# A table of 670 urgencies in place of lines of urgency, with an early table load and later small loads

## The chip, the cores and the metric

The kernel runs on one core of a Trainium2 chip. The metric is device time in microseconds from launch to end. Before the change the median of three timed runs is 1019.95 us (1019.66 to 1020.05).

## What is computed

Attention with a threshold, then two MLPs, all in float32 at the interface. Batch 4, 8 heads, 576 positions, head width 64; so 2304 tokens of width 512, and a hidden width of 2048.

```python
scores = scale * np.matmul(q, k.transpose(0, 1, 3, 2))
thresh = np.max(scores, axis=-1, keepdims=True) - tau
scores = np.where(scores >= thresh, scores, -1000000000.0)
attn = np.exp(scores - np.max(scores, axis=-1, keepdims=True))
attn = attn / (np.sum(attn, axis=-1, keepdims=True) + 1e-09)
x = np.matmul(attn, v)                    # to (B * S, H * D)
g = s * np.maximum(x @ moe_w_in, 0.0) ** 2 + b
x = g @ moe_w_out
h = x @ moe2_w_in
out = (h * (1.0 / (1.0 + np.exp(-1.702 * h)))) @ moe2_w_out
```

## The kernel before

**Work.** Attention goes by batch, half of the query rows (256, the last half with the 64 left over) and pair of heads. A tile is 128 queries of one head. For it TensorE forms the scores with k negated and scaled (`scores`, L491), VectorE takes the least of a row (`nm`, L515), ScalarE the exponential (L537), and VectorE masks and sums (L541). In the first two halves ("f32") the result is transposed on TensorE (L552) and evicted by ScalarE; in the other six it is split in two f16 parts by ScalarE and GpSimd (L565, L566) and transposed by a DMA (L568). Then comes the product with v (L636).

Weights arrive as f32 and are brought to the form in which f16 products are exact enough: a cast (`convert`, L774, by ScalarE or VectorE through `copy`, L335 and L339), a shift (L778), a norm of the weights (L812 to L822, on TensorE and VectorE), and a split in two f16 halves with a common scale (`split_w`, L341 and L863). The first 256 rows go through the first MLP in f32 (`pair32` L1004, `bank32` L1036), the other units of 256 rows as three f16 products (`pair` L977, `bank` L1065). The second MLP works on blocks of 512 rows with seven products in place of eight for the first matrix (`hidden7`, L1277; `hidden2`, L1333, for the last block) and plain ones for the second (`rows2`, L1364).

**Order.** The program is straight-line code. The class `Plan` collects steps, each with its engines, its costs in ns, what it reads and writes, and an urgency `prio`. `Plan.run` (L125) goes through time by these costs: whenever an engine is free it takes the ready step of lowest `prio`, and steps that may run on two engines go to the one that would end them first. `emit` then writes the instructions in that order. So every engine works off a fixed order, and an instruction whose input is late holds what stands behind it. SyncE, which issues all DMAs, is one of these queues.

The urgency of a step comes from the table `KN`: for attention from a start and a pace for each half batch (`a0`, `p0`, ...; `attention`, L693), for the MLPs from a start and a pace for each stage (`mlp`, L1382). The steps that a single call of `do`, or a single job of `mlp`, adds have one such value; here they are called a group.

**Parts near the change.** `consts` (L299) loads tau, s and b, one number each for all 128 partitions, ahead of everything. k's scale is made from tau; s and b are used by the first MLP only. `bank_of` (L827) hands out PSUM banks for the MLPs: one, `y`, until the time `wide`, then three in turn. `scale_out` (L921) finds the common scale of an output matrix and splits its 16 slices.

Of the kernel before, what the change touches and what calls it, by code (L numbers as in the profile page):

```python
# [9 lines left out]
F32 = mybir.dt.float32  # L10
# [39 lines left out]
}  # L50

# [22 lines left out]
class Plan:  # L74
# [6 lines left out]
    def __init__(self):  # L81
        self.steps, self.free, self.turns, self.segment = [], {}, {}, 0
        self.prio, self.first, self.bufs = 0.0, 0.0, []

    def add(self, engines, fn, reads=(), writes=(), allocs=None, prio=None, turns=False):
# [6 lines left out]
        op["prio"] = (self.prio if prio is None else prio) - self.first * ("PE" in engines)  # L92
        op["segment"] = self.segment
# [181 lines left out]
def act(cols, psum=False):  # L275
    return cols * 0.834 + (53.0 if psum else 93.0)
# [12 lines left out]
class Kernel:  # L289
# [9 lines left out]
    def consts(self, pool):  # L299
# [28 lines left out]
    def copy(self, dst, src, reads, writes, cols, scale=None, psum=False, also=0, **kw):  # L328

        nc = self.nc  # L330

        def fn(e):
            if e == "DVE":
                if scale is None:
                    nc.vector.tensor_copy(dst(), src())  # L335
                else:
                    nc.vector.tensor_scalar(dst(), src(), scale(), None, ALU.mult)
            elif scale is None:
# [3 lines left out]
        self.plan.add(self.some({"ACT": act(cols, psum) + (93 if callable(scale) else 0), "DVE": dve(cols, True, psum)}, also), fn, reads, writes, **kw)  # L342
# [29 lines left out]
    def prep_qk(self, p):  # L372
# [15 lines left out]
        add({"ACT": act(S) + 93.0}, lambda _: nc.scalar.activation(k.ap, k.ap, AF.Copy, scale=self.qs), [k], [k])  # L388

    def most(self, b, hp, rv):  # L390

        if hp == 0:
            self.mx[b] = self.at("mx", [P, H], F32, 2)
        mx = self.mx[b]
        self.plan.add(
            {"DVE": float(dve(640))},
            lambda _: self.nc.vector.tensor_reduce(
                mx[:, 2 * hp : 2 * hp + 2], rv.ap, AX.X, ALU.max, apply_absolute_value=True
            ),
            [rv], [(mx, hp)],  # L400
        )
# [42 lines left out]
    def prep_v(self, p):  # L444
# [17 lines left out]
        for h in range(2):  # L462
# [3 lines left out]
                {"DVE": dve(376)},  # L466
# [30 lines left out]
    def tile_step(self, p, i):  # L497
# [22 lines left out]
        if plain:  # L520
            add(
                {"POOL": 300.0},
# [3 lines left out]
        else:  # L526
            add(
                {"DVE": 130.0},
# [7 lines left out]
            {"ACT": 624.0},  # L536
# [25 lines left out]
        self.copy(lambda: p16[:, :S], lambda: e.ap, [e], [(p16, 0)], S)  # L562
# [4 lines left out]
        add({"POOL": Shared(pool(MAIN) + pool(H2))}, low, [e, (p16, 0)], [(p16, 1)])  # L567
        add({"SP": (1360.0, 1800.0, 1280.0)}, lambda _: nc.sync.dma_start_transpose(pt(), p16.ap), [p16], [(PT, part)], turns=True)  # L568

    def finish_sums(self, p):  # L570
# [28 lines left out]
        for h in range(2):  # L599
# [7 lines left out]
            self.copy(lambda h=h: rs[h * H2 : (h + 1) * H2], lambda rT=rT: rT.ap, [rT], [(rs, h)], n, psum=True)  # L607
# [85 lines left out]
    def attention(self, pairs):  # L693
# [3 lines left out]
        for n, p in enumerate(pairs):  # L697
# [4 lines left out]
            def do(step, p, i):  # L702
# [3 lines left out]
                plan.prio = at  # L706
                self.lending = p["b"] * NP + p["hp"] < KN["lend"]
# [57 lines left out]
    def convert(self, m, f, which, stage):  # L765
# [8 lines left out]
        self.copy(lambda: tw[:, :, 1], lambda: st[:, 4:2052:4].bitcast(BF16), [st], [tw], 512, also=KN["cast"])  # L774
# [163 lines left out]
    def bias(self):  # L938
# [11 lines left out]
        for i0 in range(KD):  # L950
# [7 lines left out]
            [C, sv["U"]], [sv["b"]],  # L958
# [33 lines left out]
    def pair32(self, u, jp):  # L992
# [22 lines left out]
        if jp % 2 == 0:  # L1015
# [7 lines left out]
            [gt], [(g, k)],  # L1023
# [27 lines left out]
    def bank(self, u, ib):  # L1051
# [6 lines left out]
        for h in range(2):  # L1058
# [16 lines left out]
            if (ib, h) == (0, 0):  # L1075
# [8 lines left out]
                if u["at"] == 0 or u["n"] == KN["fu"]:  # L1084
                    add(self.tiny(2), scale, [sv["U"], (self.ub, b)], [(sv["y"], b)])
# [296 lines left out]
    def mlp(self):  # L1382
# [189 lines left out]
```

## Time and profile before

| | |
|---|---|
| median of the timed runs | 1019.95 us |
| the profiled execution, its own time | 1023.23 us |
| its span, first to last instruction | 1021.5 us |
| TensorE busy | 979.0 us, 96% |
| VectorE, ScalarE, GpSimd busy | 694.9, 622.8, 207.3 us |
| mean granted clock of TensorE | 0.992 |

In the profile PE is TensorE, PEld its weight loads, DVE VectorE, ACT ScalarE, POOL GpSimd, SPq the queue of SyncE. Names are out<-in, L is a line of the kernel, and what stands in brackets is the idle time of that engine just before and what ended it. The clock is the share of full speed that was granted: 1.00 is 2.4 GHz, and a mean below it says that part of the stretch ran at 1.2 GHz. The trace shows each f32 product as two matmuls where the program has one, and a score tile as four.

### The profile page before, as it was taken

To read this page: it belongs to the slowest core of one execution; us is meant where nothing else is said; L and a number is where in the kernel's file an instruction comes from. 1 tells how busy PE (TensorE), PEld (TensorE's weight loads), DVE (VectorE), ACT (ScalarE), POOL (GpSimd) and SP (SyncE) were. 2 spreads that over 40 slices of the span, in tenths; PEclk is the share of its full clock that TensorE was granted. 3 is DMA by queue.
4 is the path that set the end of the run, shared out by engine and by line. 5 is a ranking of instruction groups with operands and counts; after the bars stand their busy time and mean duration, and the time that the engine had idled before them with its cause. 6 is when DMAs were issued, how large, how long until landed. Compare 5 with 4: busy or idle time off the path is not lost.

```text
span 1021.5 us, 21133 instructions
## 1 busy us (share of the span) xinstructions
PE 979.0 (96%) x8181; PEld 723.0 (71%) x8181; DVE 694.9 (68%) x1538; ACT 622.8 (61%) x1194; POOL 207.3 (20%) x319
## 2 busy tenths in 40 slices
PE   5888999979999999999999999999999999999998
PEld 3556667757877777777778888886486486486483
DVE  5888688796778777886675888796366356356240
ACT  5777776587677666676555888694364355354250
POOL 2110034433443454444442000000001001000000
PEclk9999999999999999999999999999999999999999
DMA  7786267736668786776764257310010010000000
GB/s 258 260 287 220 68 167 176 172 66 160 123 136 210 157 165 126 151 169 144 148 105 83 93 175 237 131 49 1 32 53 1 31 53 1 31 32 1 31 12 21
DMA packets 173060, 115.84 MB, mean 113 GB/s; under 512 B 136536, under 2 KB 149920, under 8 KB 172960
## 3 DMA queue, kind: packets, MB, share of 16 engines
q1 hardware_dynamic: 172960, 114.50, 43.8%
q8 instruction: 64, 1.05, 0.4%
q14 instruction: 36, 0.29, 0.1%
HBM read 72.62 MB, written 10.00 MB: 81 GB/s over the span
## 4 chain that ended last, share of the span: by engine, by line
PE 74%; DVE 10%; ACT 7%; DMA 5%; issue 2%; POOL 0%; SPq 0%; ACTq 0%; DVEq 0%; POOLq 0%
PE a L1364 18%; PE yy L1065 11%; PE a L1277 8%; PE yy L977 7%; PE S L491 6%; PE y L977 4%; PE T L636 3%; PE y L1036 3%; PE yy L1277 3%; PE d L1277 2%; DVE e L541 2%; DMA wst<-in_moe_w_out 2%; DMA PT<-p 2%; DVE nm L515 2%; PE y L1277 2%
## 5 line engine op out<-in xcount | busy, mean ns | idle before, releaser
L977 PEld LDWEIGHTS <-wb 128*128 128x128 f16 x1536 | 147.8, 98 | 32.8 <-issue 15.9
L565 POOL TENSOR_TENSOR p<-e,p 128x512 f16<-128x512 f32 x108 | 128.5, 1190 | 204.3 <-ACT p L339 176.6
L1065 PEld LDWEIGHTS <-wb 128*128 128x128 f16 x1536 | 148.5, 98 | 26.7 <-issue 9.3
L1065 PE MATMUL yy<-g,wb 128*128 128x256 f16 x1248 | 146.3, 274 | 2.1 <-DVE g L354 1.7
L541 DVE SCALAR_TENSOR_TENSOR e<-S,tb,e 128x576 f32<-128x576 f32 x144 | 115.0, 814 | 47.4 <-ACT e L537 44.0
L1364 PE MATMUL a<-wb,g 128*128 128x512 f16 x648 | 145.2, 379 | 0.0
L1277 PEld LDWEIGHTS <-l 128*128 128x128 f16 x1344 | 131.5, 98 | 19.2
L515 DVE TENSOR_REDUCE nm<-S 128x1 f32<-128x576 f32 x144 | 104.5, 749 | 29.9 <-PE S L491 29.7
L1364 PEld LDWEIGHTS <-g 128*128 128x128 f16 x648 | 63.4, 98 | 72.1
L537 ACT ACTIVATE e<-S,tb 128x576 f32<-128x576 f32 x108 | 76.4, 735 | 56.7 <-DVE tb L529 47.1
L977 PE MATMUL yy<-xs,wb 128*128 128x256 f16 x888 | 104.2, 273 | 0.0
L1277 PE MATMUL a<-xs,l 128*128 128x256 f16 x768 | 96.4, 273 | 0.0
L339 ACT ACTIVATE p<-e 128x576 f16<-128x576 f32 x108 | 73.0, 677 | 32.9 <-DMA PT<-p 22.8
L977 PE MATMUL y<-xs,wb 128*128 128x256 f16 x648 | 78.6, 273 | 7.3 <-ACT gt L984 7.3
L341 ACT ACTIVATE gt<-a,x2y 128x512 f32<-128x512 f32 x18 | 12.4, 688 | 88.0 <-PE a L1364 64.8
L354 POOL TENSOR_TENSOR st<-wb 128x512 f32<-128x512 f32 x5 | 7.1, 1418 | 276.3 <-DVE gt L1234 123.0
L491 PE MATMUL S<-kk,qa 64*128 64x288 f32 (+1 forms) x320 | 54.6, 445 | 8.2 <-ACT kk L388 8.2
L1229 ACT ACTIVATE gt<-wb,x2h 128x256 f32<-128x256 f32 x64 | 36.4, 609 | 40.4 <-DVE wb L1296 37.8
L491 PE MATMUL S<-kk,qb 64*128 64x288 f32 (+1 forms) x320 | 57.6, 453 | 1.5 <-DVE e L541 1.4
L1289 ACT ACTIVATE wb<-a 128x256 f32<-128x256 f32 x96 | 36.3, 379 | 30.2 <-PE a L1277 29.7
L778 DVE SCALAR_TENSOR_TENSOR wb<-wst,tw 128x512 int32<-128x512 int32 x64 | 45.5, 713 | 6.6 <-ACT tw L339 6.0
L1364 PE MATMUL a<-wb 128*128 128x512 f16 x216 | 49.4, 379 | 0.0
(184 smaller groups left out, 1589.2 us busy)
## 6 DMA issues: line engine op xcount, KB each, us to landing
wst<-in_moe_w_in SPq DMA_DIRECT2D x32, 512.0 KB
wst<-in_moe_w_out SPq DMA_DIRECT2D x32, 512.0 KB
rv<-in_v SPq DMA_DIRECT2D x32, 320.0 KB
kk<-in_k SPq DMA_DIRECT2D x32, 288.0 KB
qb<-in_q SPq DMA_DIRECT2D x16, 288.0 KB
yd<-gt SPq DMA_DIRECT2D x18, 256.0 KB
wb<-yd SPq DMA_DIRECT2D x16, 256.0 KB
out<-gt SPq DMA_DIRECT2D x16, 256.0 KB
```

The costliest lines, as they stand in the source:

```text
L339: nc.scalar.activation(dst(), src(), AF.Copy)
L491: nc.tensor.matmul(Sp[to, half, :HALF], q[h][r, qcols], k[r, h * HALF : (h + 1) * HALF])
L515: {"DVE": 668.0}, lambda _: nc.vector.tensor_reduce(nm.ap, Sv(), AX.XY, ALU.min), [Sp], [nm],
L537: lambda _: nc.scalar.activation(ev(), Sv(), AF.Exp, bias=nm.ap if plain else nb(), scale=-1.0), [Sp, biased], [e],
L541: lambda _: nc.vector.scalar_tensor_tensor(ev(), Sv(), tb(), ev(), ALU.is_le, ALU.mult, accum_out=p["acc"][:, i, 0:1]),
L565: nc.gpsimd.tensor_tensor(p16[:, S + H2 :], e[:, :MAIN], p16[:, :MAIN], ALU.subtract)
L778: lambda _: nc.vector.scalar_tensor_tensor(stage[:, j, :].bitcast(I32), st.ap.bitcast(I32)[:, 1:1025:2], 13, flat(), ALU.logical_shift_rig ...
L977: nc.tensor.matmul(hps[:, h, :], W[:, i, j, kk * P : (kk + 1) * P], x[:, k, kk, :], start=t == 0, stop=t == len(terms) - 1,)
L1065: nc.tensor.matmul(yp[:, h, :], self.W[0, 1, c][:, i, j, i0 * P : (i0 + 1) * P], u["g"][c][:, k, j, :], start=t == 0, stop=t == len(terms) ...
L1229: lambda _, cols=cols, h=h: nc.scalar.activation(gt[:, cols], h(), AF.Tanh, scale=th[:, c : c + 1]),
L1277: nc.tensor.matmul(to(bank), W[:, u, m, j, kk * P : (kk + 1) * P], y[:, v, z, kk, :], start=n == 0 and not more, stop=n == 5, skip_group_c ...
L1364: nc.tensor.matmul(yp(), part(f, k), self.W[1, 1, f // CH][:, w, f % CH, :], start=n == 0, stop=n == 47,)
```

## The change

1. Each group of steps gets an urgency of its own: a table `MOVES` of 670 numbers, in units of 100 ns, one for each group in the order in which the program forms them (the first ones attention's, the later ones those of the MLPs), is added to the value that the line gives. `KN` keeps its lines.
2. Costs of some steps in the plan are changed: the cast of weights and some copies on ScalarE by 50 to 180 ns, the scale of k by 67, the exponential from 624 to 650, `tb` from 130 to 200 on VectorE with a port shared with GpSimd, and others alike. They change the order only.
3. `consts` loads tau only, and calls an exponential on a column of ones, so that ScalarE's table load stands first on it. s and b are loaded by steps of the first `prep_qk`, behind the first k and q; what uses them now waits for a buffer `scal`.
4. Some steps may go to GpSimd (`tp`, `kp`, `mp`); all three switches are 0.

```diff
+MOVES = [
+    -17, -87, -158, 439, -1, -284, -28, 285, -1, 61, -158, -163, -103, -293, -250, -322, -101, 289, 151, 1356, -464,
...
+]
...
+        op["prio"] += 100.0 * MOVES[self.group] if self.group < len(MOVES) else 0.0
+        op["group"] = self.group
...
-        for i, src in enumerate((self.tau, self.s, self.b)):
-            nc.sync.dma_start(sc[:, i : i + 1], src.partition_broadcast(P))
-        self.s_ap, self.b_ap = sc[:, 1:2], sc[:, 2:3]
+        self.scal = Buf(None, "scal", None, None)
+        nc.sync.dma_start(sc[:, 0:1], self.tau.partition_broadcast(P))
+        warm = pool.tile([P, 1], F32, name="warm")
+        nc.scalar.activation(warm, self.ones[:, 0:1], AF.Exp)
+        self.scal_t, self.s_ap, self.b_ap = sc, sc[:, 1:2], sc[:, 2:3]
...
-        add({"ACT": act(S) + 93.0}, lambda _: nc.scalar.activation(k.ap, k.ap, AF.Copy, scale=self.qs), [k], [k])
...
+        engines = {"ACT": act(S) + 160.0}
...
+        add(engines, scale, [k], [k])
+        if p["unit"] == p["hp"] == 0:
+            for i, src in ((1, self.s), (2, self.b)):
+                self.load(lambda i=i: self.scal_t[:, i : i + 1], lambda src=src: src.partition_broadcast(P), [self.scal], P * 4)
...
-                {"DVE": dve(376)},
+                {"DVE": dve(490)},
...
-                {"DVE": 130.0},
+                {"DVE": Shared(200.0)},
...
-            {"ACT": 624.0},
+            {"ACT": 650.0},
...
                 plan.prio = at
+                plan.group += 1
...
             self.plan.prio = t
+            self.plan.group += 1
```

The queue of SyncE at the start of the program, before the change (`kk`, `qa` and `qb` are k and q, `wst` a slice of weights):

```order
L311 DMA scal<-in_tau 128x1
L311 DMA scal<-in_moe_s 128x1
L311 DMA scal<-in_moe_b 128x1
L358 DMA kk<-in_k 128x576
L358 DMA qa<-in_q 128x256
L358 DMA qb<-in_q 128x256
L358 DMA wst<-in_moe_w_in 128x2048
L358 DMA kk<-in_k 128x576
L358 DMA qa<-in_q 128x256
L358 DMA qb<-in_q 128x256
```

and with it:

```order
L350 DMA scal<-in_tau 128x1
L404 DMA kk<-in_k 128x576
L404 DMA qa<-in_q 128x256
L404 DMA qb<-in_q 128x256
L404 DMA scal<-in_moe_s 128x1
L404 DMA kk<-in_k 128x576
L404 DMA qa<-in_q 128x256
L404 DMA qb<-in_q 128x256
L404 DMA wst<-in_moe_w_in 128x2048
L404 DMA scal<-in_moe_b 128x1
```

The first k and q moved up by two places, s behind them, b behind the first weights; the second k and q moved ahead of the first weights.

ScalarE at the same place, before (`tw` is a cast of weights, `e` the exponential, `PT` an eviction of transposed tiles):

```order
L388 ACT_TABLE_LOAD
L388 ACTIVATE kk<-kk,qs 128x576
L339 ACTIVATE tw_78<-wst 128x512
L537 ACTIVATE e<-S,nm 128x576
L388 ACTIVATE kk<-kk,qs 128x576
L537 ACTIVATE e<-S,nm 128x576
L339 ACTIVATE PT_177<-TP 128x4x128
L339 ACTIVATE PT_177<-TP 64x128
```

and with the change:

```order
L352 ACT_TABLE_LOAD
L352 ACTIVATE warm<-ones 128x1
L437 ACTIVATE kk<-kk,qs 128x576 x2
L598 ACTIVATE e<-S,nm 128x576
L382 ACTIVATE tw_78<-wst 128x512
L598 ACTIVATE e<-S,nm 128x576
L382 ACTIVATE PT_178<-TP 128x4x128
L382 ACTIVATE PT_178<-TP 64x128
```

The table load stands alone with its call, and both first copies of k ahead of the first exponential.

TensorE at the norm of the first group of weights, which ends near 84 us, before (`TP` are transpositions, `T` small ones of the sums, L820 the norm's small product, L1004 the f32 matmuls of the first MLP, on the same bank `y`):

```order
L552 MATMUL TP<-ident,e 128x128 x4
L552 MATMUL TP<-ident,e 64x128
L820 MATMUL y<-ident,n_935 128x128
L1004 MATMUL y<-xs,wb 128x256 x4
L552 MATMUL TP<-ident,e 128x128 x4
L552 MATMUL TP<-ident,e 64x128
L605 MATMUL T<-ident,ri 64x128 x2
L491 MATMUL S<-kk,qa 128x288 x2
L491 MATMUL S<-kk,qa 64x288 x2
L491 MATMUL S<-kk,qb 64x288 x2
```

and with the change, where the same lines are L613, L666, L882 and L1066:

```order
L613 MATMUL TP<-ident,e 128x128 x4
L613 MATMUL TP<-ident,e 64x128
L552 MATMUL S<-kk,qa 128x288 x2
L666 MATMUL T<-ident,ri 64x128 x2
L882 MATMUL y<-ident,n_1019 128x128
L613 MATMUL TP<-ident,e 128x128 x4
L613 MATMUL TP<-ident,e 64x128
L666 MATMUL T<-ident,ri 64x128 x2
L1066 MATMUL y<-xs,wb 128x256 x4
L672 MATMUL T<-ident,ri 128x128
L552 MATMUL S<-kk,qa 64x288 x2
```

Transpositions and two small ones now stand between the norm's product and the f32 matmuls.

TensorE at the scale of the last v, near 433 us, before (L416 and L428 turn the maxima of v and spread the scale; rows of weight loads alternate with the matmuls):

```order
L1065 MATMUL yy<-g,wb 128x256
L1065 LDWEIGHTS wb
L1065 MATMUL yy<-g,wb 128x256
L428 MATMUL T<-dg,ones 128x8
L1065 LDWEIGHTS wb
L1065 MATMUL yy<-g,wb 128x256
```

and with the change, the same end of the stretch between them:

```order
L1039 LDWEIGHTS wb
L1039 MATMUL y<-xs,wb 128x256
L1039 LDWEIGHTS wb
L1039 MATMUL y<-xs,wb 128x256
L552 MATMUL S<-kk,qa 128x288 x4
L489 MATMUL T<-dg,ones 128x8
L1039 LDWEIGHTS wb
```

Two score tiles (L552, four matmuls) now stand just ahead of the spread, behind twelve matmuls as before.

## Rows read from the trace of the kernel before

**Rows 1.** Busy time by stretch: us, then each engine's busy time (count), TensorE's clock, DMA.

```profile
0.00:8.17 8.17, 0.00 (x0) 0.00 (x1) 0.62 (x6) 2.06 (x2) 2.71 (x11) 1.00 0.53 165
8.17:100.00 91.83, 78.81 (x495) 50.00 (x497) 78.09 (x174) 70.48 (x141) 11.12 (x35) 0.94 0.78 270
100.00:200.00 100.00, 97.25 (x745) 72.62 (x743) 77.93 (x190) 67.92 (x127) 30.16 (x51) 1.00 0.58 141
200.00:235.00 35.00, 26.17 (x278) 20.24 (x275) 31.37 (x66) 28.16 (x53) 12.59 (x15) 1.00 0.37 73
...
390.00:440.00 50.00, 47.67 (x509) 36.84 (x508) 40.76 (x94) 31.59 (x55) 23.80 (x35) 1.00 0.69 140
...
600.00:650.00 50.00, 47.86 (x438) 42.50 (x437) 40.03 (x73) 40.36 (x83) 1.27 (x1) 1.00 0.58 198
650.00:1000.00 350.00, 350.00 (x2441) 238.70 (x2439) 190.84 (x410) 172.08 (x362) 8.37 (x6) 1.00 0.08 27
1000.00:1021.50 21.50, 16.71 (x78) 7.34 (x76) 0.00 (x0) 1.37 (x2) 0.00 (x0) 0.95 0.11 24
```

**Rows 2.** Whom TensorE waited for, whole span: us in total, times, longest.

```profile
PE y L977 <- ACT gt L984: 7.3, 5, 2.4
...
PE y L1004 <- DVE n L822: 2.7, 2, 2.3
```

**Rows 3.** Timeline of the start: start us, us, engine, line, operation, idle before it.

```profile
1.20 0.42 SPq L311 DMA_DIRECT2D scal<-in_moe_s  x1
...
2.13 0.43 SPq L358 DMA_DIRECT2D kk<-in_k  x1
...
6.05 1.28 ACT L388 ACT_TABLE_LOAD   x1 [6.05 <-DMA kk<-in_k]
...
7.34 0.77 ACT L388 ACTIVATE kk<-kk,qs 128x576 f32<-128x576 f32 x1
...
8.17 2.29 PE L491 MATMUL S<-kk,qa 64*128 64x288 f32 x8 [8.17 <-ACT kk L388]
```

**Rows 4.** Timeline around 84 us, TensorE.

```profile
83.61 0.77 PE L552 MATMUL TP<-ident,e 128*128 128x128 f32 x5
...
84.21 0.27 PE L820 MATMUL y<-ident,n 128*128 128x128 f32 x1
...
86.75 2.89 PE L1004 MATMUL y<-xs,wb 128*128 128x256 f32 x8 [2.27 <-DVE n L822]
```

**Rows 5.** Timeline around 433 us, TensorE.

```profile
431.00 1.47 PE L1065 MATMUL yy<-g,wb 128*128 128x256 f16 x12
...
433.45 0.38 PE L428 MATMUL T<-dg,ones 8*128 8x8 f32 x2 [0.98 <-DVE dg L425]
...
435.95 0.76 PE L491 MATMUL S<-kk,qb 64*128 64x288 f32 x4
```

**Rows 6.** Timeline from 202 to 212 us, all engines.

```profile
202.74 1.16 POOL L565 TENSOR_TENSOR p<-e,p 128x512 f16<-128x512 f32 x1
...
208.44 2.56 ACT L341 ACTIVATE wb<-wb,o 128x512 f16<-128x512 f32 x4 [2.06 <-DVE o L930]
...
210.12 3.63 DVE L863 SCALAR_TENSOR_TENSOR wb<-wb,o 128x512 f16<-128x512 f32 x4
...
211.47 0.57 ACT L984 ACTIVATE gt<-y 128x512 f32<-128x512 f32 x1
...
211.65 1.55 POOL L565 TENSOR_TENSOR p<-e,p 128x512 f16<-128x512 f32 x1 [4.43 <-ACT p L339]
...
212.10 0.82 PE L977 MATMUL y<-xs,wb 128*128 128x256 f16 x6 [2.43 <-ACT gt L984]
```

**Rows 7.** TensorE's groups by line and form: busy us, mean ns, idle before.

```profile
L1004 PE MATMUL y<-xs,wb 128*128 128x256 f32 x128 | 32.0, 396 | 2.7 <-DVE n L822 2.7
...
L812 PE MATMUL y<-wb 128*128 128x128 bf16 x128 | 8.7, 219 | 0.6 <-DVE n L822 0.6
```

**Rows 8.** Busy time by stretch, 75 to 100 us.

```profile
75.00:100.00 25.00, 22.40 (x159) 15.47 (x159) 20.77 (x47) 19.86 (x42) 1.85 (x7) 0.93 0.71 243
```

More of the change, by code (lines that the diff above doesn't have):

```diff
@@ L82, in __init__ @@
         self.steps, self.free, self.turns, self.segment = [], {}, {}, 0
-        self.prio, self.first, self.bufs = 0.0, 0.0, []
+        self.prio, self.first, self.bufs, self.group = 0.0, 0.0, [], -1
     def add(self, engines, fn, reads=(), writes=(), allocs=None, prio=None, turns=False):
@@ L325, in consts, with copy @@
         nc.vector.memset(self.offs[:, 1:2], LOG_SP)
-    def copy(self, dst, src, reads, writes, cols, scale=None, psum=False, also=0, **kw):
+    def copy(self, dst, src, reads, writes, cols, scale=None, psum=False, also=0, wide=False, more=0.0, **kw):
         nc = self.nc
@@ L337, in fn @@
                     nc.vector.tensor_scalar(dst(), src(), scale(), None, ALU.mult)
+            elif e == "POOL":
+                nc.gpsimd.tensor_copy(dst(), src())
             elif scale is None:
@@ L341, in fn @@
                 nc.scalar.activation(dst(), src(), AF.Copy, scale=scale if isinstance(scale, float) else scale())
-        self.plan.add(self.some({"ACT": act(cols, psum) + (93 if callable(scale) else 0), "DVE": dve(cols, True, psum)}, also), fn, reads, writes, **kw)
+        engines = self.some({"ACT": act(cols, psum) + (93 if callable(scale) else 0) + more, "DVE": dve(cols, True, psum)}, also)
+        if wide:
+            engines["POOL"] = pool(cols, True)
+        self.plan.add(engines, fn, reads, writes, **kw)
     def some(self, engines, i):
@@ L387, in prep_qk, with scale @@
             )
-        add({"ACT": act(S) + 93.0}, lambda _: nc.scalar.activation(k.ap, k.ap, AF.Copy, scale=self.qs), [k], [k])
+        def scale(e):
+            if e == "ACT":
+                nc.scalar.activation(k.ap, k.ap, AF.Copy, scale=self.qs)
+            else:
+                nc.gpsimd.tensor_scalar(k.ap, k.ap, self.qs, None, ALU.mult)
+        engines = {"ACT": act(S) + 160.0}
+        if KN["kp"]:
+            engines["POOL"] = pool(S, True)
+        add(engines, scale, [k], [k])
+        if p["unit"] == p["hp"] == 0:
+            for i, src in ((1, self.s), (2, self.b)):
+                self.load(lambda i=i: self.scal_t[:, i : i + 1], lambda src=src: src.partition_broadcast(P), [self.scal], P * 4)
     def most(self, b, hp, rv):
@@ L394, in most @@
         mx = self.mx[b]
+        engines = {"DVE": float(dve(640))}
+        if KN["mp"]:
+            engines["POOL"] = pool(640, True)
         self.plan.add(
-            {"DVE": float(dve(640))},
-            lambda _: self.nc.vector.tensor_reduce(
+            engines,
+            lambda e: self.eng[e].tensor_reduce(
                 mx[:, 2 * hp : 2 * hp + 2], rv.ap, AX.X, ALU.max, apply_absolute_value=True
@@ L561, in tile_step @@
         p16 = self.at("p16", [P, 2 * S], F16, KN["pb"], KN["lp"])
-        self.copy(lambda: p16[:, :S], lambda: e.ap, [e], [(p16, 0)], S)
+        self.copy(lambda: p16[:, :S], lambda: e.ap, [e], [(p16, 0)], S, more=50.0)
         def low(_):
@@ L606, in finish_sums @@
             add({"PE": pe(2 * T, P)}, turn, [ri], [rT])
-            self.copy(lambda h=h: rs[h * H2 : (h + 1) * H2], lambda rT=rT: rT.ap, [rT], [(rs, h)], n, psum=True)
+            self.copy(lambda h=h: rs[h * H2 : (h + 1) * H2], lambda rT=rT: rT.ap, [rT], [(rs, h)], n, psum=True, more=90.0)
         if not p["last"]:
@@ L773, in convert @@
         self.turns += 1
-        self.copy(lambda: tw[:, :, 1], lambda: st[:, 4:2052:4].bitcast(BF16), [st], [tw], 512, also=KN["cast"])
+        self.copy(lambda: tw[:, :, 1], lambda: st[:, 4:2052:4].bitcast(BF16), [st], [tw], 512, also=KN["cast"], wide=KN["tp"], more=180.0)
         flat = lambda: tw.ap.rearrange("p a b -> p (a b)").bitcast(I32)
@@ L1084, in bank @@
                 if u["at"] == 0 or u["n"] == KN["fu"]:
-                    add(self.tiny(2), scale, [sv["U"], (self.ub, b)], [(sv["y"], b)])
+                    add(self.tiny(2), scale, [sv["U"], (self.ub, b), self.scal], [(sv["y"], b)])
         for h in range(2):
```

8 lines of the change are left out of this document (4 added, 4 removed), and 34 rows, old and new, of tables (KN, MOVES).

## The prediction

> **What bounds the kernel now.** I read the table of stretches first [rows 1]. From 650 to 1000 us TensorE is busy 350.00 of 350 us: there the matmuls set the pace, and an order of steps can neither gain nor hide anything. The holes lie ahead of it: 8.17 us before the first matmul, 13.0 us between 8.17 and 100 (91.83 less 78.81), 2.75 between 100 and 200, 8.8 between 200 and 235, 2.3 between 390 and 440, 2.1 between 600 and 650, and 4.8 in the tail, where the last eviction and store follow the last matmul. Together that is 42 of the 42.5 us for which TensorE is idle in the 1021.5 us span. The same table shows the granted clock at 0.94 from 8.17 to 100 us and at 1.00, the level of 2.4 GHz, in the next hundred: 0.06 x 91.83 = 5.5 us of full speed lost to pieces at 1.2 GHz, where TensorE has its holes. From 8.17 to 100 VectorE is busy for 85% of the time (78.09 of 91.83), from 100 to 200 for 78%, and TensorE's idle share falls with it, from 14.2% to 2.75%.
>
> Then the list of who TensorE waited for [rows 2], and the timeline at the places it names. At the start [rows 3] the first k waits in the queue behind three loads of one number each; its landing releases a table load on ScalarE, and only after that is k scaled. At 84 us [rows 4] a small product is put ahead of a group of f32 matmuls that needs the same bank, and TensorE waits 2.27 us for VectorE in between. At 433 us [rows 5] it waits 0.98 us for VectorE's scale of the next v. After 206 us [rows 6] six hidden groups of the first MLP use one bank in turn, and each must be evicted by ScalarE, which has blocks of four weight copies (2.56 us) in its order.
>
> **The change part by part.** The sum is made against the profiled execution (1023.23 us, span 1021.5) and applied to the median of the timed runs, 1019.95; they stand 0.3% apart, which moves a sum of 10 us by 0.03.
>
> *Start: 2.2 us.* The changed order puts k behind tau alone. It takes the slot at 1.20 that the load of s has now, 0.93 us ahead of 2.13 [rows 3]. It landed at 6.05, so 5.12 now. The table load (7.34 less 6.05, 1.28 us) is now released by a constant that GpSimd writes among its first instructions, so nothing stands between the landing and the copy: 5.12 + 0.77 + the 0.06 us hop = 5.95 in place of 8.17. Bounds: 1.28 if the landing does not move, 2.2. The loads of s and b are read by the first MLP alone, much later, and cost a slot of 0.47 us each (half of 0.93) behind the first k and q. The second k's copy now stands before the first exponential on ScalarE; if that k came late the exponential would wait, which is the 0.9 us bound on the other side. By the Trainium skill, "ScalarE: Activation LUTs", What ACT_TABLE_LOAD costs, a table load is followed by a drain and comes to about 2.66 us; the trace shows the copy beginning 7.34 less 6.05 = 1.29 us after the load began, with no drain, so I keep the row. By the page the term would be 1.4 us more and the sum 1009.3.
>
> *The product at 84 us: 0.8 us.* In the new order five transpositions stand between the small product and the f32 group; they take 0.77 us [rows 4] and fill that much of the 2.27 us. Bounds 0 and 2.27.
>
> *The scale of v at 433 us: 1.0 us.* Two score tiles now stand beside the twelve matmuls that fill the wait; one takes 0.76 us [rows 5], so 1.5 us cover the whole 0.98. Bounds 0 and 0.98. The holes of 600 to 650 I leave.
>
> *The f32 attention up to about 140 us: 3.5 us.* Ahead of VectorE's 36th masking product the order now has 171 instructions in place of 187; at 78.09 us for 174 [rows 1] each is 0.45, so 7.2 us of its work goes later. Ahead of TensorE's last f32 transposition stand 16 fewer f32 MLP matmuls and 16 fewer of the weight norm: 16 x 32.0/64, since the trace splits each of the 64 in two, and 16 x 8.7/128 [rows 7], 9.1 us. If VectorE sets the pace, the stretch ends 7.2/0.85 = 8.5 us sooner, and the 9.1 us come back later: +0.6. If the hole follows VectorE's load, as between the two stretches above, 7.2 of some 110 us takes the load from 85 to 79.5% and the idle share from 14.2 to 5.3%, 8.1 us. If the chain of one tile sets the pace, nothing ends sooner and 9.1 us come back. I take the middle of the first two, since the waits are spread over VectorE and ScalarE; bounds -8.1 and +9.1.
>
> *Clock: 1.75 us.* One fall of the clock lies around the 2.27 us hole: 0.93 over 75 to 100 us is 25 x 0.07 = 1.75 [rows 8]. A hole cut to 1.5 us and a stretch with fewer of them should keep this one up. Bounds 0 and the whole 5.5; one fall more would cost 1.75.
>
> *The clump at 206 to 232 us: 0.* Its one bank stays, the four blocks of four copies stay, and on ScalarE the relu of each group still stands behind such a block. Three more score tiles are finished ahead of it, but one more copy of k stands in it. Bounds -7.3 (all waits gone) and +8.4 (below). Two subtractions move from VectorE to GpSimd; beside VectorE's weight subtractions one of GpSimd's takes 1.55 us against 1.16 elsewhere [rows 6], so at most 0.4 us each on an engine nobody waits for, and six casts go from VectorE to ScalarE where both have gaps: nothing. The Trainium skill, "SBUF — State Buffer", Who interferes with whom, has the two engines block each other for whole instructions, which speaks against the move; the trace agrees in direction (1.55 against 1.16). By that rule each of the two could hold VectorE for a whole 1.55 us, 3.1 us in all, and the sum would be 1013.8.
>
> Sum: 2.2 + 0.8 + 1.0 + 3.5 + 1.75 = 9.25 us, so 1019.95 - 9.25 = 1010.7.
>
> **The rivals.** *Only the start is won.* The order shifts holes about: what leaves the f32 stretch comes back later. For it: the moved matmuls are as long (9.1 us) as the time that VectorE saves (8.5). Against it: 100 to 200 us shows that the same mixture runs with 2.75 us of holes. 1019.95 - 2.2 = 1017.7.
>
> *The holes close.* All idle between 8.17 and 200 us goes (15.8), with the clock's 5.5, the start's 2.2 and the 4.4 of 390 to 440 and 600 to 650; the clump stays. 27.9 us, 992. For it: the stretch from 650 to 1000 runs without a hole, with VectorE at 55%. Against it: at 85% VectorE leaves little room, and a tile's chain from score to transposition is as long as before.
>
> *The clump grows: slower.* In it TensorE waited five times for ScalarE, 7.3 us in all [rows 2]. If every group meets a whole block, each wait is 2.56 + 0.57 = 3.13 us [rows 6], 15.7 in all, 8.4 more. With the start's 2.2 and nothing else, 1026. It makes the kernel slower once the five waits pass 9.5 us (1.9 each) if only the start is won, or 16.5 us if everything else comes as summed. For it: relu and block still alternate. Against it: the score tiles finished ahead take work out of this stretch.
>
> **How the numbers follow.** Forecast 47%, its own range 1004 to 1016; only the start 20%; holes close 20%; clump grows 13%. A difference of 0.2% (2.04 us) is about what a measurement of this kernel can tell from none. The start alone is at that edge, so I split it 11 faster and 9 same: faster 0.47 + 0.20 + 0.11 = 0.78, same 0.09, slower 0.13. For the range I leave out half of the closing holes below 995, and most of the growing clump above 1021.
>
> **What would show it.** Right: the first matmul near 5.95 us with the table load at 1 us; a wait under 1.6 us between the norm's small product and the f32 group; TensorE's idle between 8 and 200 us at 9 to 12 us; the clock above 0.95 there; five waits on ScalarE of about 7 us after the weight scale is known; no hole from 650 us on. Wrong: idle of 20 us or more up to 235 us (the order only moved it), waits for relu above 2 us each, or new waits on weight loads. If the last blocks, which now mix hidden groups with output rows, showed holes, the tail would be the step that I did not price.

## The result: slower by 0.6%

The changed kernel takes 1024.37 us (median of five runs, 1022.68 to 1027.16), the kernel before in the same session 1019.66. The ratio is 1.006, 95% interval 1.0041 to 1.0079: 4 to 8 us slower, where 9.25 us less was forecast.

The profile after is of an execution of 1024.37 us. The table of stretches, with the columns and almost the stretches of [rows 1] (core 0: span of the stretch, busy time of PE, PEld, DVE, ACT, POOL, granted clock, DMA share, GB/s):

```profile
0.00:8.17 8.17, 2.29 (x8) 1.19 (x8) 1.38 (x7) 2.84 (x4) 2.89 (x12) 1.00 0.66 186
8.17:100.00 91.83, 78.60 (x524) 47.65 (x524) 80.84 (x180) 73.09 (x146) 14.23 (x37) 0.98 0.77 268
100.00:200.00 100.00, 96.89 (x710) 72.30 (x709) 77.00 (x187) 69.25 (x128) 31.83 (x53) 1.00 0.68 151
200.00:235.00 35.00, 26.90 (x277) 20.65 (x275) 32.56 (x76) 28.25 (x50) 13.58 (x18) 1.00 0.44 93
390.00:440.00 50.00, 50.00 (x517) 39.94 (x516) 35.52 (x94) 33.99 (x60) 23.16 (x32) 1.00 0.72 142
440.00:600.00 160.00, 156.41 (x1546) 128.35 (x1544) 113.52 (x249) 100.44 (x183) 50.26 (x68) 0.99 0.54 122
600.00:650.00 50.00, 48.15 (x436) 42.24 (x434) 42.33 (x78) 37.85 (x78) 5.60 (x4) 1.00 0.55 185
650.00:1000.00 350.00, 350.00 (x2425) 236.66 (x2423) 183.77 (x401) 164.15 (x353) 1.67 (x1) 1.00 0.08 29
```

TensorE's idle time from 8.17 to 200 us is 16.3 us (13.2 and 3.1); it was 15.8. The 2.3 us of 390 to 440 are gone. Between 440 and 600, where it had not stood still at all in the first profile of the kernel before, it now idles 3.6 us; a second profile of the kernel before, shown below, idles 2.3 us there. The list of whom TensorE waited for, to be held against [rows 2] (total us, times, longest):

```profile
PE TP L613 <- ACT PT L382: 6.2, 8, 1.6
PE y L1039 <- ACT gt L1046: 5.8, 5, 2.0
PE yy L863 <- ACT sq L849: 2.0, 1, 2.0
PE y L1211 <- DVE x2t L1208: 1.3, 1, 1.3
```

The wait of 2.27 us at 84 us has left the list, and the five waits on the one bank have shrunk from 7.3 to 5.8. The waits of f32 transpositions for ScalarE's evictions have grown to 6.2 us, from 2.1 and 2.0 in the two profiles of before, and two waits on small products of the second MLP's scales are new (2.0 and 1.3). Around the first of the new ones, TensorE, and below it ScalarE (start us, us, instruction, and in brackets the idle time before it):

```profile
588.65 2.78 PE L1039 MATMUL y<-xs,wb 128*128 128x256 f16 x24
591.27 1.48 PE L1039 MATMUL yy<-xs,wb 128*128 128x256 f16 x12
594.71 0.39 PE L863 MATMUL yy<-fro,ones 128*128 128x4 f32 x2 [1.96 <-ACT sq L849]
594.95 5.76 PE L1127 MATMUL yy<-g,wb 128*128 128x256 f16 x36
```

```profile
591.80 0.79 ACT L382 ACTIVATE tw<-wst 128x512 f16<-128x512 bf16 x1
592.79 0.60 ACT L1046 ACTIVATE gt<-yy 128x512 f32<-128x512 f32 x1 [0.20 <-PE yy L1039]
593.41 0.63 ACT L1047 ACTIVATE gt<-gt 128x512 f32<-128x512 f32 x1
593.95 0.61 ACT L849 ACTIVATE sq<-wb 128x512 bf16<-128x512 f32 x1
```

The small product needs a square of the weights that stands on ScalarE behind a cast and the two steps of an eviction. The 36 matmuls behind the hole take 5.76 us, where at the pace of the 24 in the first line (2.78) they would take 4.2: part of them runs at 1.2 GHz, and the granted clock from 595 to 601 us is 0.72.

### The profile page after: what moved, and what is told of

It is laid out like the page before. It is cut to its first block, busy times and chain, and to the rows that moved or that the text cites. A ratio compares the mean times of both kernels' runs of the same rounds, so it can differ in the third digit from the quotient of the medians.

```text
span 1022.6 us, 21121 instructions
## 1 busy us (share of the span) xinstructions
PE 980.6 (96%) x8181; PEld 721.3 (71%) x8181; DVE 686.5 (67%) x1532; ACT 620.4 (61%) x1199; POOL 211.5 (21%) x321
## 3 DMA queue, kind: packets, MB, share of 16 engines
q8 instruction: 64, 1.05, 0.4%
## 4 chain that ended last, share of the span: by engine, by line
PE 78%; DVE 9%; DMA 5%; ACT 5%; issue 2%; SPq 1%; POOL 0%; DVEq 0%; ACTq 0%; POOLq 0%
PE a L1426 18%; PE yy L1127 10%; PE a L1339 8%; PE S L552 7%; PE yy L1039 7%; PE T L697 5%; PE y L1039 4%; PE y L1127 3%; PE y L1098 3%; PE yy L1339 3%; PE d L1339 2%; PE y L1066 2%; PE y L1339 2%; DVE l L955 2%; PE yy L1395 1%
## 5 line engine op out<-in xcount | busy, mean ns | idle before, releaser
L1039 PEld LDWEIGHTS <-wb 128*128 128x128 f16 x1536 | 148.1, 98 | 33.1 <-issue 15.3
L1039 PE MATMUL yy<-xs,wb 128*128 128x256 f16 x888 | 106.5, 273 | 1.6 <-ACT gt L1046 1.3
L552 PE MATMUL S<-kk,qa 64*128 64x288 f32 (+1 forms) x320 | 55.0, 448 | 6.5 <-ACT kk L437 5.7
L552 PE MATMUL S<-kk,qb 64*128 64x288 f32 (+1 forms) x320 | 57.0, 453 | 3.0 <-DVE e L602 2.9
L1291 ACT ACTIVATE gt<-wb,x2h 128x256 f32<-128x256 f32 x64 | 37.5, 608 | 21.8 <-DVE wb L1358 20.8
L400 DVE TENSOR_TENSOR g<-gt,g 128x512 f16<-128x512 f32 x53 | 43.9, 833 | 8.3 <-ACT g L382 7.8
```

The source lines that it names most:

```text
L552: nc.tensor.matmul(Sp[to, half, :HALF], q[h][r, qcols], k[r, h * HALF : (h + 1) * HALF])
L1039: nc.tensor.matmul(hps[:, h, :], W[:, i, j, kk * P : (kk + 1) * P], x[:, k, kk, :], start=t == 0, stop=t == len(terms) - 1,)
```

## The experiments

Ratios are to the kernel before in the same session (17 to 35 runs of it), with 95% intervals; a ratio that is 0.0001 higher is 0.1 us more. A single execution can lie up to some 8 us from the median of its kernel, the kernel before ranging from 1014.6 to 1029.2 over all sessions.

**A second profile of the kernel before (e0).** No edit.

> The kernel before, unchanged, profiled a second time. Its first profiled execution was 1023.23 us with a span of 1021.5, 3.6 us above the median of the timed runs, so its span beside that of the changed kernel (1022.6) shows a loss of 1.1 us only, where the timed runs show 4 to 5. If the first profiled execution was a long one by chance, this span is about 1017 to 1018 and some hole of the first is smaller. If profiling itself adds 3 us to this kernel, it is 1021 again.

1018.49 us, span 1016.7. So the first profile was a long execution. The second one's stretches from 8.17 to 100 and from 440 to 600 us:

```profile
8.17:100.00 91.83, 81.36 (x522) 50.46 (x523) 79.58 (x178) 73.65 (x146) 12.73 (x36) 0.96 0.79 270
...
440.00:600.00 160.00, 157.74 (x1574) 130.17 (x1572) 115.56 (x255) 105.82 (x191) 47.38 (x68) 1.00 0.58 126
```

In the first it has 10.5 us of idle time in place of 13.0 and a clock of 0.96 in place of 0.94 [rows 1], with the same instructions. In the second it idles 2.3 us, all of them between 580 and 600, where the first profile had none. So that stretch was full in one execution only. The loss of the change is to be read against this one: 5.9 us of span, not 1.1.

**The start alone (e1).** The order of before, the table load early, s and b issued behind the q of the first pair of heads (the code that issues them there is left out):

```diff
-        for i, src in enumerate((self.tau, self.s, self.b)):
-            nc.sync.dma_start(sc[:, i : i + 1], src.partition_broadcast(P))
+        nc.sync.dma_start(sc[:, 0:1], self.tau.partition_broadcast(P))
+        warm = pool.tile([P, 1], F32, name="warm")
+        nc.scalar.activation(warm, self.ones[:, 0:1], AF.Exp)
...
```

> The order of the kernel before, with the early table load and with the two small loads behind the first q. Theory 1 (the start is won and then given back within the first 25 us, because the matmuls run at 1.2 GHz until about 21.7 us in the changed kernel): first S at about 5.8 us, but at 25 us of the span TensorE is only 0.3 to 0.6 us of work ahead, and the time is 0 to 0.6 us under that of before. Rival (the start's 2.4 us stay won wherever the order is the old one): 1017.3 to 1017.7. The other rival (the early start makes the f32 stretch worse): slower by 1 us or more.

The ratio is 1.0001 (0.9986 to 1.0017): nothing is won. The first scores start at 5.75 us, but the first transposition at 13.13, later than the 12.11 of before (second profile). ScalarE's timeline, and then the row of 5 to 7 us, whose last two numbers are the DMA engines' share and GB/s:

```profile
4.93 0.78 ACT L398 ACTIVATE kk<-kk,qs 128x576 f32<-128x576 f32 x1 [2.69 <-DMA kk<-in_k]
10.78 0.77 ACT L341 ACTIVATE tw<-wst 128x512 f16<-128x512 bf16 x1 [5.08 <-DMA wst<-in_moe_w_in]
11.42 0.71 ACT L547 ACTIVATE e<-S,nm 128x576 f32<-128x576 f32 x1
```

```profile
5.00:7.00 2.00, 1.25 (x6) 0.97 (x8) 0.00 (x0) 0.70 (x1) 0.00 (x0) 1.00 0.43 81
```

The cast of the first weight block stands ahead of the first exponential on ScalarE and waits 5.08 us for its load. While the two small loads pass, the queues move 81 GB/s.

**The start with the small loads late (e4).** As e1, against which the diff stands, but s and b are issued behind the second q of the third pair of heads, at 15.3 us:

```diff
-            if h and p["unit"] == p["hp"] == 0:
+            if h and p["unit"] == 0 and p["hp"] == 2:
```

> The start-only kernel again (order of before, early table load), but with the two small loads issued behind the second q of the third pair of heads, some 20 us or more in. Theory 1a (a load of one number to 128 partitions holds up what stands behind it in the queue far longer than the slot of 0.47 us: in the start-only kernel the first weight block landed 2.5 us later than before and held up ScalarE's order): first weight block back at about 8 us or earlier, first transposition at 9.8 to 10.3 us in place of 13.1, time 1016.5 to 1017.5. Rival (the first tiles are bound by matmuls at 1.2 GHz until about 20 us, whatever lands): first transposition earlier, but 1018 to 1019 as the start-only kernel.

The ratio is 0.9966 (0.9945 to 0.9986), faster than both kernels. The same two views:

```profile
4.91 0.78 ACT L398 ACTIVATE kk<-kk,qs 128x576 f32<-128x576 f32 x1 [2.68 <-DMA kk<-in_k]
6.91 0.78 ACT L341 ACTIVATE tw<-wst 128x512 f16<-128x512 bf16 x1 [1.22 <-DMA wst<-in_moe_w_in]
7.91 0.74 ACT L547 ACTIVATE e<-S,nm 128x576 f32<-128x576 f32 x1 [0.22 <-DVE nm L525]
```

```profile
5.00:7.00 2.00, 1.26 (x6) 0.98 (x8) 0.00 (x0) 0.78 (x2) 0.00 (x0) 1.00 1.03 390
```

The block is there 3.9 us earlier, 390 GB/s pass, and the first transposition starts at 9.65. Up to 12 us the queues carry 307 packets under 512 B here and 573 in e1; the two loads of one number to 128 partitions are the only difference between the runs.

**The changed order with either start (e2, e5).** e2 puts the old start under the changed order (the diff of e1 backwards, and the planned loads of s and b issue nothing); e5 is the changed kernel with s and b at e4's place.

> The changed order, with the start of the kernel before (three small loads ahead of the first k, no early table load). Theory 2 (the order itself costs the 4 to 5 us, by new holes between 440 and 600 us with a fall of the clock, and the start gives little): 1024 to 1027, that is 0 to 2.4 us above the changed kernel. Rival (the early start upsets an order that would be good with the old one): at or below the kernel before, 1016 to 1020.

> The changed kernel in its order, with the two small loads at the same late place. Theory 1a: the second k lands before 7 us in place of 7.5 and the first weight block ahead of 9.6; 1022.5 to 1023.8, 0.5 to 2 us under the changed kernel. Rival (the loss of the changed kernel lies in its order alone): the same as the changed kernel within 0.5 us.

The ratios are 1.0074 (1.0049 to 1.0099) and 1.0034 (1.0013 to 1.0055). So the order costs 0.7% under either start: e2 against the kernel before, e5 against e4. The start as the change has it (1.006) lies between, 1.4 us under e2 and 2.6 above e5. With intervals of 2 us and more, and from several sessions, neither difference is clear of noise; the 4 us between e2 and e5 just are.

What the start does under the changed order is seen better where the same instruction runs in two executions. The f32 transpositions of e2 and e5 (count; shortest, median and longest ns; first and last start in us), to be held against 10.0 and 119.2 in the changed kernel:

```profile
L613 PE MATMUL TP<-ident,e x180: 272/273/477, 12.1 to 122.3; 128*128 128x128 f32 x144, 128*64 128x128 f32 x36
```

```profile
L622 PE MATMUL TP<-ident,e x180: 272/273/476, 9.7 to 117.2; 128*128 128x128 f32 x144, 128*64 128x128 f32 x36
```

Under the changed order the first one starts 2.1 us earlier with the change's start than with the old one, and the late small loads bring only 0.3 us more.

**The durations without the table (e3).**

```diff
-        op["prio"] += 100.0 * MOVES[self.group] if self.group < len(MOVES) else 0.0
+        op["prio"] += 100.0 * MOVES[self.group] if self.group < 0 else 0.0
```

> The changed kernel with its table of urgencies left at zero; the higher durations that the planner is given and the new start stay. Theory 3 (the higher durations make the order worse and the table wins most of it back): 1030 to 1045, with more holes than the changed kernel in the f32 stretch and in the clump at 206 to 232 us. Rival (the table is what costs time): 1016 to 1021, about the kernel before.

The ratio is 1.0228 (1.0204 to 1.0251). The longer durations, with the lines of urgency as they were, give an order that is 23 us slower; the table wins 17 of them back. The table with the old durations was not run. TensorE from 440 to 650 us:

```profile
440.00:600.00 160.00, 150.06 (x1491) 120.61 (x1488) 107.85 (x248) 97.81 (x171) 60.53 (x84) 0.95 0.58 123
600.00:650.00 50.00, 45.29 (x386) 39.14 (x387) 43.34 (x84) 40.75 (x82) 5.72 (x4) 0.93 0.43 148
```

**Both orders side by side (c1, c2).** Order and engine of every step written out as a table, one for each order, both with e4's start (the tables themselves are left out):

```diff
...
-            (order,) = plan.run(engines)
+            order = ORDER
+            for op in plan.steps:
+                op["on"] = {"p": "PE", "d": "DVE", "a": "ACT", "g": "POOL", "s": "SP"}[ON[op["n"]]]
```

> Control: the whole order of before with the small loads late, instruction for instruction the kernel that measured 0.9966 of the kernel before. If that holds: 0.9945 to 0.9986. If it was chance: 0.999 or more.

> Control: the whole changed order with the small loads late, the kernel that measured 1.0034. If the order itself costs 5 us or more: 1.002 to 1.006, and 5 to 8 us above the control with the order of before. Rival (the orders are equal and the sessions differ): within 2 us of that control.

The ratios are 0.9971 (0.9951 to 0.9992) and 1.0037 (1.0019 to 1.0056). Both repeat what e4 and e5 gave; the order costs 6.7 us (some 4 to 9 by the intervals) with nothing else changed. Part of it is the choice of engine, which differs for 100 of the 4200 steps.

Where it costs them can be read from the work done. I counted the matmuls of each kind in a stretch, gave each its time at 2.4 GHz, and took the sum from the stretch. What is left is lost: to idle time, to the low clock, or to matmuls that follow one another more slowly than that. The last is no small part, since from 235 to 500 us c1 idles 2.8 us at a clock of 1.00 and yet loses 21.8. In us:

```
stretch      before,2nd   after    c1     c2
0 to 25         18.0       17.6   16.3   17.6
25 to 100       16.4       18.9   16.8   19.5
100 to 235      19.9       20.8   20.7   21.2
235 to 500      21.3       18.2   21.8   18.3
500 to 550       2.5        3.1    2.6    2.9
550 to 650       2.2        7.3    3.0    7.3
sum             80.3       85.8   81.2   86.7
```

Up to 500 us the orders come out nearly even (75.6 in c1, 76.6 in c2), the changed one losing 4.5 ahead of 235 us and winning 3.5 behind it. From 550 to 650 it loses 4.3. Each column is one execution. All twelve executions with the old order in this last stretch lose 0.7 to 4.9 us there, all seven with the changed one 5.8 to 8.8. Counted in the same way, the two orders are also apart in every execution from 235 to 500 us. Ahead of 235 us their executions overlap, so the loss there is less sure.

**The orders joined (h1 to h4, y1, y2).** At some times the two orders have done the same steps but for two to nine. There the table of one can be continued with that of the other: `ORDER` is the first part of one, then what is left in the order of the other. The times that name the joints are the planner's, some us off those of the trace.

> The two orders agree in all but 4 steps on what is done by 507 us of the changed plan, so they can be joined there. Changed order up to 507 us, order of before from there on; start with the small loads late in this and the next three (kernel with the order of before and that start: 0.9966 of the kernel before; changed order and that start: 1.0034). Theory 2b (the loss of the order lies wholly behind 507 us, in 550 to 650): 0.993 to 0.998 of the kernel before. Rival (the loss is spread, or lies in the f32 stretch): 1.000 to 1.004.

> Order of before up to 507 us, changed order from there on. Theory 2b: 1.001 to 1.005, the whole loss of 4 to 5 us between 550 and 650. Rival: 0.996 to 0.999, no loss.

> Changed order up to 179 us (where the two differ in 2 steps), order of before from there on. This holds the stretch of f32 attention that the prediction gave 3.5 us, the product at 84 us (0.8) and the clock (1.75). As predicted: 0.990 to 0.992, 4 to 6 us under the same start with the order of before. Rival (nothing is won there): 0.9956 to 0.998. Rival (it loses, by the waits of transpositions for ScalarE at 84 and 88 us): 0.999 or more.

> Order of before up to 179 us and from 507 us on, changed order between. It holds the clump at 206 to 232 us (predicted 0) and the scale of v at 433 us (1.0 us). As predicted: 0.995 to 0.997. Rival (the changed order costs 2 us or more here): 0.9985 or more.

The ratios are 1.0003 (0.9985 to 1.0022) for h1, 1.0021 (1.0000 to 1.0043) for h2, 1.0005 (0.9986 to 1.0024) for h3 and 1.0034 (1.0013 to 1.0056) for h4. Against the mean of the two runs of the old order, 0.9969, the changed order from 507 us on costs 5.3 us (h2) and up to 179 us 3.7 (h3), each with an error of some 2.5. h1 has a wait of 2.0 us at its joint, so some 1.5 of its 3.5 us are the order's, less than the error. h4 cannot be read, because its first joint is a hole with a fall of the clock (0.58 from 191 to 198 us, 16 f32 matmuls in 6.20 us in place of 3.62):

```profile
187.94 1.54 PE L830 MATMUL S<-kk,qa 64*128 64x288 f32 x8 [1.34 <-issue]
...
191.20 0.64 PE L944 MATMUL T<-ident,ri 128*64 128x128 f32 x2 [1.39 <-ACT rs L651]
191.63 6.20 PE L1376 MATMUL y<-g,wb 128*128 128x256 f32 x16
```

> Small loads late; order of before up to 159 us (where the two orders differ in 3 steps) and from 477 us on (4 steps), changed order between. Theory (the changed order is the better one there, by the scale of v at 433 us and the evictions around it, and loses elsewhere): 0.993 to 0.9955 of the kernel before, where the order of before throughout measured 0.9966 and 0.9971. Rival (the gain seen in the profiles is bought by work put off, and comes back behind 477 us): 0.9965 to 0.999. If a joint makes a hole again as in the run of 179 to 507 us: above 1.000.

> The same with the first joint at 200 us (9 steps differ). Theory: 0.993 to 0.9955; rival 0.9965 to 0.999; a hole at a joint: above 1.000, seen as a wait of TensorE at 195 to 210 us.

The ratios are 1.0010 (0.9990 to 1.0030) and 1.0015 (0.9993 to 1.0036). Again the joints cost: in y1 TensorE stands still for 3.3 us ahead of 172 us, which neither order alone does, and lost time from 200 to 235 us is 15.2 in y2 where c1 has 9.7. Between 235 and 500 us both lost 2 to 4 us less than c1, as c2 does, but no run has kept that as time. Neither beats c1.

**Why 550 to 650 us (e7, x1).** e7 moves two steps of the changed order back on TensorE, with what depends on them: the norm's small product of 594.7 us behind the next 12 matmuls, the transposition of 645.5 us behind the next 30 (the function that moves them is left out).

```diff
             (order,) = plan.run(engines)
+            order = later(plan.steps, order, 2805, 2829)
+            order = later(plan.steps, order, 3020, 2987)
...
```

> The changed kernel with two small products moved back on TensorE: the one of the norm at 594.7 us behind the next twelve matmuls of the output group, the transposition of 645.5 us behind the next thirty. Theory 2a (both small products stand too early in the order, their waits of 1.96 and 1.34 us and the fall of the clock behind the first, 1.8 us, are the price of that): both waits gone, 3 to 5 us under the changed kernel, 1019.5 to 1021.5. Rival (ScalarE and VectorE are busy 18 of 20 us there, so the output group meets its own operands late and the wait comes back behind the first twelve matmuls): 0 to 1.5 us under it.

The ratio is 1.0038 (1.0014 to 1.0062), against 1.006 in another session: 2 us, which the intervals don't tell apart from none. The wait came back in pieces. From 585 to 645 us:

```profile
PE yy L863 <- ACT gt L1046: 1.4, 1, 1.4
PE yy L1039 <- DVE xs L1187: 1.2, 2, 0.7
PE yy L1039 <- ACT xs L384: 1.0, 2, 0.6
PE yy L863 <- ACT sq L849: 0.7, 1, 0.7
```

That is 4.3 us, on both engines, where the changed kernel has 2.3 in the same stretch (1.96 and 0.3) and 1.3 at 645.5 us, which e7 has not. So it is not the place of these two products alone; that ScalarE's and VectorE's work is late there is the likely reading. From 580 to 600 us ScalarE is busy 18.1 and VectorE 17.9 of 20 us in the changed kernel, 16.0 and 16.2 in the second profile of before.

x1 takes up the other suspect. The changed order gives GpSimd five subtractions between 560 and 650 us that VectorE has in the old one. In the changed kernel, GpSimd and then VectorE:

```profile
637.70 1.27 POOL L400 TENSOR_TENSOR st<-wb 128x512 f32<-128x512 f32 x1 [61.88 <-DMA wst<-in_moe_w_out]
639.05 1.34 POOL L400 TENSOR_TENSOR wb<-wb 128x512 f32<-128x512 f32 x1
640.46 1.33 POOL L400 TENSOR_TENSOR st<-wb 128x512 f32<-128x512 f32 x1
```

```profile
637.94 2.73 DVE L376 CAST g<-gt 128x512 f16<-128x512 f32 x2
640.59 2.35 DVE L400 TENSOR_TENSOR g<-gt,g 128x512 f16<-128x512 f32 x2
```

Two casts take 2.73 us and two subtractions 2.35; one cast takes 0.43 and one subtraction 0.68 elsewhere. The Trainium skill, "SBUF — State Buffer", Who interferes with whom, has the two engines share a pair of ports, and the trace agrees: 2.9 us of VectorE are lost. x1 puts the five back (`ON` "d" in place of "g" for five steps).

> The changed order with the small loads late, and the five subtractions that it gives to GpSimd between 560 and 650 us back on VectorE, where the order of before has them. Around 640 us two casts took 2.73 us on VectorE beside GpSimd's subtractions and 0.86 without, two subtractions 2.35 and 1.37. Theory 2c (this contention makes a good part of the loss of 550 to 650 us): VectorE's casts back at 0.43 us, the waits of 640 to 648 us gone, 2 to 3 us under the control with the changed order. Rival (VectorE is full there anyway, and now has five subtractions of 0.69 us more, 3.4 us): the same within 1 us.

The ratio is 1.0026 (1.0010 to 1.0042), 1.1 us under c2 and within the error. The wait of 1.7 us for VectorE's scale is down to 0.7, but the hole of 594 us stays with its 2.0. So the contention is there, but no more than an error's worth of time is won when VectorE does the work itself; that I gave GpSimd's added subtractions no price made no difference that can be measured.

**The low clock of the first tiles (e6, w2).** Fourteen matmuls of a constant by a constant, which compute nothing that is used, on e4:

```diff
+            hot = self.ph.tile([P, P], F32, name="hot", tag="y", bufs=1)
+            for _ in range(14):
+                nc.tensor.matmul(hot, self.ones, self.ident, start=True, stop=True)
```

> The kernel with the small loads late (order of before), with 14 matmuls of a constant by a constant ahead of the first score, which compute nothing that is used. Theory (TensorE runs the first tiles at 1.2 GHz because it did nothing before them): first scores x8 in about 1.5 us in place of 2.29, transpositions x5 in 0.75 in place of 1.33 from the first on; 0.8 to 2.5 us under the kernel without them, 1014.5 to 1016.5. Rival (the clock falls again in the idle time between the first score and the first transposition): the first scores alone are faster, 0 to 0.8 us.

The ratio is 0.9979 (0.9957 to 1.0000). They ran behind the first scores, from 7.99 to 13.04 us, and held the first transposition up by 3.4 us; so this tested something else. w2 puts ten of them into the first step of TensorE and three behind the second.

> The order of before with the small loads late, with ten matmuls of constants ahead of the first scores and three more between the second scores and the first transposition, this time at these places. Theory (TensorE runs the first tiles at 1.2 GHz because it did nothing before): scores x8 in 1.5 to 1.9 us, transpositions x5 in 0.75 from the first on, 1 to 2 us under the control with the order of before. Rival (the first tiles are bound by ScalarE's and VectorE's chain, not by matmuls): matmuls faster, time the same within 0.7 us.

The ratio is 0.9975 (0.9952 to 0.9998), as c1 (0.9971). TensorE in w2:

```profile
1.46 4.63 PE L1533 MATMUL hot<-ident,ones 128*128 128x128 f32 x20 [1.46 <-POOL ident masks.py:199]
6.02 1.37 PE L501 MATMUL S<-kk,qa 64*128 64x288 f32 x8
...
9.49 0.77 PE L562 MATMUL TP<-ident,e 128*128 128x128 f32 x5 [1.23 <-DVE e L551]
10.19 0.76 PE L501 MATMUL S<-kk,qb 64*128 64x288 f32 x4
11.95 0.74 PE L562 MATMUL TP<-ident,e 128*128 128x128 f32 x5 [1.01 <-DVE e L551]
```

The clock is up, by the durations: the first scores take 1.37 us where they took 2.29 in c1, the transpositions 0.77 where they took 1.33. The clock column cannot show it, since it reads 1.00 from 5 to 7 us in e1 and e4 too, with scores of 2.29 us. But each group of transpositions now waits for VectorE's masked product, and the first two start at 9.49 and 11.95 us against 9.64 and 12.16 in c1. The first tiles are bound by the chain through VectorE and ScalarE.

## Why the prediction was wrong

Two steps of the sum failed: the f32 attention, where a gain of 3.5 us was forecast and a loss came, and the stretch from 550 to 650 us, which was put at nothing and lost 4.3. The clock's 1.75 us could not be told from chance.

**Start, 2.2 us: it came under the changed order, by the traces.** The first matmul began at 5.74 us, 2.43 earlier [rows 3], with the table load at 0.73 and the exponential behind it at 2.02, right at its end: the row's 1.28 us without a drain held. The first transposition kept 2.1 us of it (10.0 against 12.1 in e2); the timed ratios, 1.4 us apart, are too coarse to confirm that. What was mis-sized is "a slot of 0.47 us each" for the loads of s and b. That is what they take to issue, and ahead of k it is nearly all they cost: k was there at 6.05 us in the kernel before [rows 3] and at 4.91 in the changed one, 1.14 us where the two slots make 0.93. Behind the first q, in e1, they made the first weight block land 3.9 us later than in e4, and there ScalarE had its cast ahead of the first exponential, so nothing was won. In the changed order the exponential stands ahead of that cast, and s stands ahead of the second k, whose copy came at 7.59 us against 6.34 in e5. That is the mechanism that I had priced at 0.9 us; it cost the first transposition 0.3.

**The f32 attention, 3.5 us: the failed step is the middle between two rules.** The stretch did end sooner. Last f32 transposition, second profile of before and changed kernel, then c1 and c2, which have the same start (columns as for e2 above):

```profile
L552 PE MATMUL TP<-ident,e x180: 272/273/474, 12.1 to 125.8; 128*128 128x128 f32 x144, 128*64 128x128 f32 x36
```

```profile
L613 PE MATMUL TP<-ident,e x180: 272/273/478, 10.0 to 119.2; 128*128 128x128 f32 x144, 128*64 128x128 f32 x36
```

```profile
L891 PE MATMUL TP<-ident,e x180: 272/273/477, 9.6 to 124.3; 128*128 128x128 f32 x144, 128*64 128x128 f32 x36
```

```profile
L891 PE MATMUL TP<-ident,e x180: 272/273/477, 9.7 to 119.8; 128*128 128x128 f32 x144, 128*64 128x128 f32 x36
```

It ended 6.6 us sooner, some 2 of them from the start; with the same start 4.5 us (c1, c2), or 7.1 if e5 is taken for c2. I had 8.5 if VectorE paced it. The 9.1 us of matmuls taken from the stretch come back behind it, so 2.0 to 4.6 us are lost: between the variant that I gave as +0.6 and the bound of +9.1. I averaged +0.6 with a variant in which idle time follows VectorE's load, and that load did not fall: from 8.17 to 119.5 us VectorE is busy 95.10 of 111.33 us in the changed kernel and 94.40 in the second profile of before, 85% in both. (Two slips besides: 7.2 of 110 us takes 85% to 78.5, not 79.5, and the middle of 8.1 and -0.6 is 3.75, not 3.5. Neither decides.) What was late instead shows in TensorE's waits between 25 and 200 us. Those for VectorE fell to 4.4 us from 7.3 (first profile) and 7.7 (second), while those for ScalarE rose to 7.7 from 5.0 and 2.0. Most of that is the eviction of transposed tiles, in the first profile of before and in the changed kernel (total us, times, longest):

```profile
PE TP L552 <- ACT PT L339: 2.1, 3, 1.2
```

```profile
PE TP L613 <- ACT PT L382: 5.9, 7, 1.6
```

The new order has tiles closer together, and the eviction of a transposed tile is what is late next. I had "the waits are spread over VectorE and ScalarE" in front of me and followed only one of them.

**The product at 84 us, 0.8.** The wait went; two waits of transpositions for ScalarE, 1.05 us at 84 and 1.63 at 88, took its place.

**Clock, 1.75.** The clock of 0.94 was that of one execution. The second had 0.96 without any change, c1 and c2 have 0.96 both, the changed kernel 0.98. This term rested on one draw.

**The scale of v at 433 us, 1.0: right.** TensorE does not idle between 390 and 440 us in the changed kernel and in c2. With the old order it waited there for VectorE's scale in four executions of five, 0.7 to 1.0 us (before, e1, e4, c1), and not in the second profile of before.

**The clump, 0: right.** 5.8 us of waits in place of 7.3 (5.9 in the second profile), idle 8.1 in place of 8.8 (6.7). The slower rival named the wrong place.

**From 550 to 650 us: put at nothing.** "The holes of 600 to 650 I leave", and a stretch that was full in one profile counted as one in which nothing could be lost. Here lie 4.3 us of the 6.7 (c1, c2) and 5.3 by the joint (h2). Shown is where it is, and that neither the place of the two small products (e7) nor GpSimd's subtractions (x1) make it alone. That ScalarE's and VectorE's work is bunched there is what the rows suggest; which of the moved steps bunch it was not tested, and stays open. So does whether the gain of 235 to 500 us can be kept.

The order by its stretches, as lost time in c2 less c1: 0 to 235 us +4.5, 235 to 500 -3.5, 500 to 650 +4.6, together 5.6 of the 6.7 us measured between them. In the changed kernel the start gave back some 2 us of that, by the traces. The sign "idle of 20 us or more up to 235 us" could not have told a moved hole from a closed one: it is 24.4 us in the changed kernel, and was 24.6 before [rows 1].

## What to carry to other kernels

A stretch in which the engine that sets the pace stood still for a moment or not at all is no stretch in which a new order can lose nothing: here it lost 4.3 us, and it must be priced like the holes. When an order puts tiles closer together to close holes, name the engine that is late next and count its waits too. And profile the old kernel twice before pricing a term of 1 or 2 us from one trace: here two executions of the same instructions differed by 2.5 us of idle time in one stretch.

## What was not expected of the hardware

- A load of one number to 128 partitions: behind the first q two of them cut the queues from 390 to 81 GB/s for two microseconds and delayed the next block by 3.9 us (e1 against e4), with 266 more packets under 512 B. Ahead of the first k the same two cost 1.14 us. Why the place matters so much was not tested. The Trainium skill, "DMA: Bandwidth & Descriptors", Rules for kernel authors, says of many small transfers that one pays mostly overhead; here it is the loads queued behind that pay.
- Matmuls of constants ahead of the first real work brought TensorE's first scores from 2.29 to 1.37 us, and the time did not change (w2).
